# Attention and a two-layer expert on one core: every engine's queue of the opening written out by hand, and per-tile exponentials for heads 4 to 7

## The chip, the cores and the metric

The kernel runs on one core of a Trainium2 chip. The metric is device time in microseconds (us), from runs of the whole program. The engines named here are TensorE (PE, its weight loads PEld), VectorE (DVE), ScalarE (ACT), GpSimd (POOL) and SyncE (SP, which issues all the DMAs). Each engine works through its own queue in order and meets the others at semaphores.

## What is computed

Windowed attention over 8 batches of 8 heads (576 positions, head dimension 64), with a plain window of 32 keys in heads 0 to 3 of a batch and a dilated one (every 4th of 128 keys) in heads 4 to 7. Its output, 4608 tokens by 512, goes through a two-layer expert with a piecewise activation. Everything is float32.

```
scores = scale * q @ k^T;  masked to the head's window
attn = exp(scores - max);  attn = attn / (sum(attn) + 1e-09)
x = (attn @ v) as (4608, 512)
h = x @ w_in                                  # 512 -> 2048
g = h where h >= 1, 0 where h <= -1, else (h + 1)^2 / 4
out = g @ w_out                               # 2048 -> 512
```

## The kernel before

Sixty-four heads are counted through all batches (head 8 is batch 1, head 0). The queries of a head are cut into 6 tiles of 96, each against 128 keys, so a head has 6 score tiles of 96x128. Heads 0 to 15 take their scores from the float32 matmul (`scores_pair`, L187, two heads at a time), later heads from operands split into a rounded part and a rest (`scores_split`, L215; `split`, L129, makes the parts on ScalarE, VectorE and GpSimd). `reduce` (L174, instructions at L176) adds the mask and takes the lowest value on VectorE, `exp` (L248) is one ScalarE exponential a tile with its sum, `whole` (L288) does it for a head at once: subtraction on GpSimd, one ScalarE exponential over 96x768, sum on VectorE. Then come the reciprocal, the scaling by it on GpSimd or VectorE, the transposes and `values` (L349), whose results are stored as a rounded part xh and a rest xl.

The expert works in 144 steps: 9 tiles of 512 tokens times 16 blocks of 128 hidden units. Step s runs `layer1` (L391, 12 matmuls of 128x512), then VectorE and ScalarE make the activation as gh and gl, and two steps later `layer2` (L426, 12 matmuls) adds it into four accumulators. `layer1` writes one of two PSUM banks (tag h), so step s needs gl of step s-2 to be finished. After the last block of a token tile four copies (ScalarE and VectorE in turn) leave the accumulators through three buffers, and four stores leave on SP's queue (L447). Weights arrive as 64-bit words and are turned into a rounded part and a rest by `weights` (L109): two ScalarE passes, a join on VectorE (L121), a rounding copy on ScalarE (L126), a difference on GpSimd (L127). All 32 blocks are converted in the first token tile.

The order: TensorE's and SP's queues follow the program text (`manual_schedule`, L553); for the other three a scheduler with priorities and a simulated time line decides (`high_priority`, `issue_after`). Attention of heads 8 and up is dealt out between the steps by `place` (L453): two slots `u` a step. From head 16 on every pair of heads takes eight steps of the stream. The split operands qs and kk, and the loaded qr and kr of these heads, have one buffer each, so head n+1's load waits for head n's split, and its split for head n's last score matmul.

```
        for s in range(len(steps) + lag):
            ...
            if s == 2:
                acc[0] = ps.tile([128, DM], F32, tag="acc0", name="acc0_0")
                spin(14, acc[0])
```

`spin` (L155) runs matmuls on a constant; nobody reads them.

Of the kernel before, what the change touches and what calls it, by code (L numbers as in the profile page):

```python
# [23 lines left out]
F32 = mybir.dt.float32  # L24
# [12 lines left out]
TOK = 512  # L37
# [6 lines left out]

@with_exitstack
def body(ctx, tc, q, k, q2, k2, v, mask, eye, w_in, w_out, out):
# [14 lines left out]
    heads = {}  # L61
# [3 lines left out]
    spare = [f"{w}{f}" for f in range(NF // 2, NF) for w in ("wi", "wo")]  # L65

    def borrow(name):
        return pool.tile([128, 2 * DM], F32, tag=spare.pop(0), name=name)

    def load_pair(n):  # L70

        if 0 < n < H:
            qr, kr = borrow(f"qr{n}")[:, :S], borrow(f"kr{n}")[:, :KPAD]
        else:
            tags = ("qs", "kk") if n % 4 else ("qr", "kr")
            qr = pool.tile([128, S], F32, tag=tags[0], name=f"qr{n}")
# [24 lines left out]
    wi, wo, raws = {}, {}, {}  # L101

    def fetch(f, src, name):

        raw = pool.tile([128, 2 * DM], U32, tag=f"{name}{f}", name=f"{name}_raw{f}")
        nc.sync.dma_start(out=raw, in_=src[:, f].bitcast(U32))
        raws[name, f] = raw

    def weights(f, w, name):  # L109

        raw = raws.pop((name, f))
        words = raw.rearrange("p (n x) -> p n x", x=2)
        low, high = words[:, :, 0], words[:, :, 1]
        m = pool.tile([128, DM], U32, tag="m", name=f"{name}_m{f}", bufs=3)
# [70 lines left out]
    def scores_pair(n, t0, t1):  # L187

        pair = (n, n + 1)
        plain = n % H < H // 2  # L190
        svs = []
        for m in pair:
            if t0 == 0:
                begin(m)
            tag, bufs = bank(n)
            sp = ps.tile([128, 512], F32, tag=tag, name=f"s{m}_{t0}", bufs=bufs)
            svs.append(sp[:QT, : (t1 - t0) * 128].rearrange("p (t j) -> p t j", j=128))
            if m == 0 and t0 == 0:
                spin(11, sp)
# [15 lines left out]
    def scores_split(n, t0):  # L215
# [3 lines left out]
        if t0 == 0:  # L219
            begin(n)  # L220
# [462 lines left out]
```

## Time and profile before

| | us |
|---|---|
| median of 3 runs | 923.7 (923.62 to 924.82) |
| the profiled execution | 924.36 |
| span of the profile, first to last instruction | 922.6 |
| TensorE busy | 903.7 (98%) |
| VectorE, ScalarE, GpSimd busy | 671.2, 493.9, 240.6 |

The profiled execution is 0.66 us above the median, and 1.76 us of it lie outside the span. TensorE's busy time counts the spins too, and its ends are modelled, so the share alone says little: what matters is when the stream of expert steps begins, and where it has gaps.

### The profile page before, as it was taken

What the parts mean: (1) busy time and instruction counts of PE and PEld (TensorE: products, weight loads), DVE (VectorE), ACT (ScalarE), POOL (GpSimd) and SP (SyncE); (2) the same over time, 40 slices, a digit from 0 to 9 for tenths busy, and PEclk for the clock granted to TensorE, in tenths of its full rate; (3) what the DMA queues carried; (4) which work ended last, traced back from release to release, by engine and by line L of the source; (5) the groups of instructions that cost most, each with busy time, mean ns of one, the idle gap of its engine ahead of it and who ended that gap; (6) DMA issues with size and microseconds to landing.
All of it is one profiled execution on the core that took longest, in us unless ns stands there. A gap on an engine that the chain in (4) does not pass through costs nothing.

```text
span 922.6 us, 14390 instructions
## 1 busy us (share of the span) xinstructions
PE 903.7 (98%) x4866; PEld 740.7 (80%) x4866; DVE 671.2 (73%) x1966; ACT 493.9 (54%) x1352; POOL 240.6 (26%) x155
## 2 busy tenths in 40 slices
PE   7889999999999999999999999999999999999997
PEld 6677788888888888888888888888888888888886
DVE  6887778878888888788888888888888643334333
ACT  6898875555555556555555565555555422222221
POOL 4575552222222322222222222222222000000000
PEclk9999999999999999999999999999999999999999
DMA  9981013221132223211322223222321010001001
GB/s 350 407 312 45 1 27 105 82 71 57 58 116 71 70 70 117 57 54 59 116 71 70 71 73 101 57 71 71 116 70 44 1 46 1 1 1 46 1 1 47
DMA packets 31018, 73.87 MB, mean 80 GB/s; under 512 B 3520, under 2 KB 3808, under 8 KB 30944
## 3 DMA queue, kind: packets, MB, share of 16 engines
q1 hardware_dynamic: 30944, 72.94, 24.4%
q8 instruction: 39, 0.64, 0.3%
q14 instruction: 35, 0.29, 0.1%
HBM read 63.49 MB, written 9.44 MB: 79 GB/s over the span
## 4 chain that ended last, share of the span: by engine, by line
PE 89%; ACT 3%; POOL 2%; DVE 2%; issue 2%; DMA 1%; DVEq 0%; POOLq 0%; ACTq 0%
PE acc L434 41%; PE h L398 40%; PE s L225 4%; PE o L360 3%; ACT c L250 1%; POOL wi L127 1%; DMA wi_raw<-w_in 1%; POOL wo L127 1%; POOL c L286 1%; DVE c L176 1%; DVE c L293 0%; PE s L159 0%; DVE xl L345 0%; ACT wi_raw L120 0%; PE s L202 0%
## 5 line engine op out<-in xcount | busy, mean ns | idle before, releaser
L434 PE MATMUL acc<-wo,gh 128*128 128x512 f32 x1152 | 382.7, 393 | 0.0
L398 PE MATMUL h<-xh,wi 128*128 128x512 f32 x1152 | 357.3, 391 | 1.2 <-DVE gl L421 1.2
L434 PEld LDWEIGHTS acc<-wo,gh 128*128 128x128 f32 x1152 | 216.5, 188 | 47.2
L398 PEld LDWEIGHTS h<-xh,wi 128*128 128x128 f32 x1152 | 209.1, 188 | 39.9 <-DVE gl L421 1.4
L434 PE MATMUL acc<-wo,gl 128*128 128x512 f32 x576 | 225.2, 391 | 0.0
L398 PE MATMUL h<-xl,wi 128*128 128x512 f32 x576 | 224.3, 389 | 0.0
L138 POOL TENSOR_TENSOR kk<-kr,kk 128x608 fp32r<-128x608 f32 x48 | 94.8, 1975 | 413.1 <-ACT kk L134 403.0
L250 ACT ACTIVATE c<-c 96x128 f32<-96x128 f32 x330 | 129.0, 393 | 121.3 <-DVE c L176 121.3
L415 ACT ACTIVATE y<-y,consts 128x512 f32<-128x512 f32 x144 | 104.2, 724 | 116.3 <-DVE y L412 116.2
L418 ACT CAST gh<-h 128x512 fp32r<-128x512 f32 x144 | 84.4, 586 | 122.4 <-PE acc L434 118.6
L412 DVE TENSOR_SCALAR y<-h 128x512 f32<-128x512 f32 x144 | 99.2, 689 | 54.7 <-PE h L398 54.3
L417 DVE TENSOR_TENSOR h<-h,y 128x512 f32<-128x512 f32 x144 | 100.5, 698 | 49.7 <-ACT y L415 48.5
L421 DVE TENSOR_TENSOR gl<-h,gh 128x512 fp32r<-128x512 f32 x144 | 98.7, 686 | 40.9 <-ACT gh L418 40.9
L398 PEld LDWEIGHTS h<-xl,wi 128*128 128x128 f32 x576 | 108.2, 188 | 23.1
L434 PEld LDWEIGHTS acc<-wo,gl 128*128 128x128 f32 x576 | 108.2, 188 | 19.6
L301 DVE STREAM_TRANSPOSE pt<-c 32x192 f32<-32x192 f32 x288 | 106.0, 368 | 7.0 <-POOL c L286 3.7
L244 DVE TENSOR_TENSOR c<-s,msk 96x256 f32<-96x256 f32 (+1 forms) x168 | 61.4, 377 | 35.5 <-PE s L225 34.5
L286 POOL TENSOR_TENSOR c<-c 96x768 f32<-96x768 f32 x56 | 83.4, 1490 | 14.4 <-DVE c L285 14.4
L176 DVE CUSTOM_DVE_ANT_0 c<-s,c 96x128 f32<-96x128 f32 x288 | 70.6, 280 | 1.0
L250 ACT ACTIVATION_READ_ACCUMULATOR c<-c 96x1 f32 x330 | 62.3, 189 | 0.0
L225 PEld LDWEIGHTS s<-kk,qs 128*96 128x96 f32 x288 | 46.3, 161 | 15.6 <-issue 0.2
L344 ACT CAST xh<-o 128x288 fp32r<-128x288 f32 (+8 forms) x112 | 38.5, 384 | 36.8 <-PE o L360 22.9
(57 smaller groups left out, 638.7 us busy)
## 6 DMA issues: line engine op xcount, KB each, us to landing
kr<-k_in SPq DMA_DIRECT2D x56, 304.0 KB, 3.3
qr<-q_in SPq DMA_DIRECT2D x56, 288.0 KB, 2.8
vt<-v_in SPq DMA_DIRECT2D x32, 384.0 KB, 3.9
out<-out SPq DMA_DIRECT2D x36, 256.0 KB, 3.3
wi_raw<-w_in SPq DMA_DIRECT2D x16, 512.0 KB, 9.5
wo_raw<-w_in SPq DMA_DIRECT2D x16, 512.0 KB, 9.5
msk<-mask_in SPq DMA_DIRECT2D x1, 144.0 KB, 4.3
ident<-eye_in SPq DMA_DIRECT2D x1, 36.0 KB, 4.4
```

Of the source, the lines that this page charges most:

```text
L138: nc.gpsimd.tensor_tensor(out=kk[:, 1], in0=hd["kr"], in1=kk[:, 0].bitcast(F32), op=ALU.subtract)
L225: PE.matmul(out=sv[:, t - t0], lhsT=hd["qs"][:, t * QT : (t + 1) * QT], rhs=hd["ks"][:, :, t * QT : t * QT + 128], start=True, stop=True,)
L250: last["act"] = nc.scalar.activation(out=c[:, t], in_=c[:, t], func=AF.Exp, bias=st[:, 0, t : t + 1], scale=-1.0, accum_out=st[:, 1, t : t ...
L286: nc.gpsimd.tensor_tensor(out=c, in0=c, in1=spread(st[:, 2]), op=ALU.mult)
L301: nc.vector.transpose(out=pt[r : r + 32, :, 32 * g : 32 * g + 32], in_=c[32 * g : 32 * g + 32, :, r : r + 32],)
L398: PE.matmul(out=hp, lhsT=wi[f][:, w, 128 * c : 128 * c + 128], rhs=x[:, c], start=c == 0 and i == 0, stop=c == NC - 1 and i == len(terms) - 1,
L412: nc.vector.tensor_scalar(out=y, in0=hp, scalar1=-1.0, scalar2=1.0, op0=ALU.max, op1=ALU.min)
L415: nc.scalar.activation(out=y, in_=y, func=AF.Square, bias=half_t, scale=0.5)
L417: activated = nc.vector.tensor_tensor(out=hp, in0=hp, in1=y, op=ALU.max)
L418: copied = nc.scalar.copy(out=gh, in_=hp)
L421: nc.vector.tensor_tensor(out=gl, in0=hp, in1=gh.bitcast(F32), op=ALU.subtract)
L434: PE.matmul(out=acc[m], lhsT=g[:, r], rhs=wo[f][:, w], start=f == 0 and i == 0, stop=f == NF - 1 and i == len(terms) - 1,)
```

## The change

A string, `OPENING`, lists some 980 operations by short names, and `play` issues them in that order with all five engines under `manual_schedule`: loads (`q0`, `wi3`), score tiles (`S0.1`), reduces (`r0.1`), exponentials (`e0.1`), conversions of weights (`a`, `b`, `j`, `h`, `l` before a block's name), quarters of `layer1` (`A2.0`) and of `layer2` (`B0.0`), spins (`W3`). It reaches through `layer1` of step 17 and `layer2` of step 15, the last of the first token tile. From there (step 18) the loop goes on as before. Functions that issued several instructions are cut into one for each. Besides:

- heads 4 to 7: six exponentials of one tile each on ScalarE in place of GpSimd's subtraction and one exponential over the head; their bias is the tile's lowest score, they take no sum, and VectorE's sum over the head stays;
- head 3's scaling goes from GpSimd to VectorE (`by_vector`);
- fixed homes for borrowed buffers (`home`), another order of the loads, other spins (28 in six places, the last ahead of the values of head 2, none ahead of step 2).

```diff
+OPENING = """
+k0 q0 msk q4 q2 k2 v0 k4 k6 S0.0 q6 S1.0 S0.1 S1.1 r0.0 S0.2 wi0 r0.1 S1.2 e0.0 S0.3 r1.0 S1.3 S0.4 r0.2 wi3
...
+j17 B15.3 S17.4 g17 m17.4 ck18 r17.5 r17.4 d17 e17.5 cl18 e17.4 i17 R17 n17 k19 q18 cq18 cs18 q19
...
-    def exp(n, t):
+    whole_pass = (8, 9, 10, 12, 14)
+    sum_apart = (4, 5, 6, 7)
+    by_vector = (3, 5, 7)
+
+    def exp(n, t=None):
         c, st = heads[n]["c"], heads[n]["st"]
-        last["act"] = nc.scalar.activation(
-            out=c[:, t],
-            in_=c[:, t],
-            func=AF.Exp,
-            bias=st[:, 0, t : t + 1],
-            scale=-1.0,
-            accum_out=st[:, 1, t : t + 1],
-        )
+        if t is None:
+            nc.scalar.activation(out=c, in_=c, func=AF.Exp, scale=-1.0)
+        else:
+            total = {} if n in sum_apart else dict(accum_out=st[:, 1, t : t + 1])
+            nc.scalar.activation(
+                out=c[:, t], in_=c[:, t], func=AF.Exp, bias=st[:, 0, t : t + 1], scale=-1.0, **total
+            )
...
+    def summed(n):
+        c, st = heads[n]["c"], heads[n]["st"]
+        nc.vector.tensor_reduce(out=st[:, 1], in_=c, op=ALU.add, axis=mybir.AxisListType.X)
...
+    def normalised(n):
+        c = heads[n]["c"]
+        engine = nc.vector if n in by_vector else nc.gpsimd
+        engine.tensor_tensor(out=c, in0=c, in1=spread(factor(n)), op=ALU.mult)
...
+    operations = {
+        "q": load_q, "k": load_k, "v": load_v,
+        "S": scores, "m": masked, "r": lowest, "z": shifted, "e": exp, "u": summed,
+        "i": guarded, "R": inverse, "n": normalised, "T": transpose_pe, "p": kept, "t": turned,
+        "V": weighted, "x": x_high, "l": x_low,
+        "cq": q_high, "ck": k_high, "cs": q_low, "cl": k_low,
+        "A": layer1, "y": clamped, "s": squared, "j": activated, "g": g_high, "d": g_low, "B": layer2,
+        "W": lambda times: spin(times, step_bank(0)),
+    }
...
+    ordered = {engines.PE, engines.SP, engines.Activation, engines.DVE, engines.Pool}
+    with tc.manual_schedule(engines=ordered):
+        for token in OPENING.split():
+            play(token)
+    lag = 2
+    with tc.manual_schedule(engines={engines.PE, engines.SP}):
+        for u in range(2 * start - 1):
+            slots.pop(u, None)
+        run(2 * start - 1)
+        for s in range(start, len(steps) + lag):
```

The order on ScalarE in the opening, first before the change. The rows run from the last exponentials of heads 2 and 3 to the end of heads 4 to 7 (c is a head's scores, t a transposed tile in PSUM, o the values, raw and m a block of weights).

```order
L250 ACTIVATE c3_176<-c3_176 96x128
L292 ACTIVATE c4_222<-c4_222 96x768
L328 COPY pts_xh_71<-t0_0_307 128x384
L292 ACTIVATE c5_224<-c5_224 96x768
L328 COPY pts_xh_71<-t1_0_322 128x384
L344 CAST xh0_367<-o0_0_360 128x288
L344 CAST xh0_367<-o0_1_371 128x224
L328 COPY pts_xh_71<-t2_0_384 128x384
L292 ACTIVATE c6_264<-c6_264 96x768
L344 CAST xh1_380<-o0_1_371 128x64
L328 COPY pts_xl_72<-t3_0_394 128x384
L292 ACTIVATE c7_266<-c7_266 96x768
```

And in the change:

```order
L354 ACTIVATE c2_place_150<-c2_place_150 96x128 x2
L178 ACTIVATE wi0_m_276<-wi0_raw_113 128x512
L354 ACTIVATE c5_place_180<-c5_place_180 96x128
L354 ACTIVATE c4_place_177<-c4_place_177 96x128
L354 ACTIVATE c2_place_150<-c2_place_150 96x128 x2
L354 ACTIVATE c4_place_177<-c4_place_177 96x128
L354 ACTIVATE c6_place_213<-c6_place_213 96x128
L354 ACTIVATE c4_place_177<-c4_place_177 96x128
L354 ACTIVATE c6_place_213<-c6_place_213 96x128 x5
L438 COPY pts_xh_71<-t0_0_286 128x384
L438 COPY pts_xh_71<-t1_0_312 128x384
L184 ACTIVATE wi0_raw_113<-wi0_raw_113 128x512
```

The four exponentials over a whole head, each of which waited for GpSimd, became tiles of several heads mixed, and the first conversions of weights stand among them.

The second place is the end of the first token tile on SP's queue. Before (qr and kr are queries and keys of a head, out0_0 to out0_3 the four stores of the first token tile):

```order
L87 DMA qr18_1622<-q2_in 128x576
L88 DMA kr18_1623<-k2_in 128x608
L96 DMA vt16_1710<-v_in 128x768
L87 DMA qr19_1763<-q2_in 128x576
L88 DMA kr19_1764<-k2_in 128x608
L447 DMA out<-out0_0_1800 128x512
L447 DMA out<-out0_1_1806 128x512
L447 DMA out<-out0_2_1812 128x512
L447 DMA out<-out0_3_1818 128x512
```

In the change:

```order
L149 DMA kr18_1670<-k2_in 128x608
L574 DMA out<-out0_0_1778 128x512
L574 DMA out<-out0_1_1788 128x512
L574 DMA out<-out0_2_1795 128x512
L574 DMA out<-out0_3_1802 128x512
L149 DMA kr19_1824<-k2_in 128x608
L135 DMA qr18_1826<-q2_in 128x576
L135 DMA qr19_1830<-q2_in 128x576
```

The load of head 18's queries moved from ahead of the four stores to behind them. On TensorE the last score matmul of head 17 (`S17.4`) moved too: before it stood ahead of `layer1` of step 17, in the change it stands behind the last matmul of `layer2` of step 15, right ahead of head 18's first score matmul.

The third place is VectorE's queue there. Before (qs is the split of the queries, pt a transposed head, gl the rest of the activation):

```order
L244 TENSOR_TENSOR c17_1697<-s17_4_1751,msk_64 96x256
L421 TENSOR_TENSOR gl1_0_1727<-h1_0_1712,gh1_0_1726 128x512
L176 ISA c17_1697<-s17_4_1751,c17_1697 96x128
L135 TENSOR_TENSOR qs18_1757<-qr18_1622,qs18_1757 64x576
L285 RECIPROCAL c17_1697<-c17_1697 96x6
L412 TENSOR_SCALAR y1_1_1789<-h1_1_1776 128x512
L444 COPY out0_1_1806<-acc0_1_769 128x512
L417 TENSOR_TENSOR h1_1_1776<-h1_1_1776,y1_1_1789 128x512
L301 STREAM_TRANSPOSE pt1_68<-c17_1697 32x6x32 x6
L244 TENSOR_TENSOR c18_1827<-s18_0_1828,msk_64 96x256
L444 COPY out0_3_1818<-acc0_3_777 128x512
```

In the change:

```order
L532 TENSOR_SCALAR y17_1782<-h1_1_1748 128x512
L571 COPY out0_1_1788<-acc0_1_747 128x512
L538 TENSOR_TENSOR h1_1_1748<-h1_1_1748,y17_1782 128x512
L571 COPY out0_3_1802<-acc0_3_764 128x512
L326 TENSOR_TENSOR c17_1726<-s17_4_1805,msk_64 96x256
L263 ISA c17_1726<-s17_4_1805,c17_1726 96x128
L549 TENSOR_TENSOR gl17_1809<-h1_1_1748,gh17_1808 128x512
L385 RECIPROCAL c17_1726<-c17_1726 96x6
L401 STREAM_TRANSPOSE pt1_68<-c17_1726 32x6x32 x6
L224 TENSOR_TENSOR qs18_1812<-qr18_1826,qs18_1812 64x576
L326 TENSOR_TENSOR c18_1841<-s18_0_1842,msk_64 96x256
```

The split of head 18's queries moved behind the fourth copy of the outputs, behind head 17's last two tiles and behind head 17's six transposes.

## Rows read from the trace of the kernel before

**Rows 1.** The page's first line.
```profile
span 922.6 us, 14390 instructions
```

**Rows 2.** Busy time by stretches, all engines. [...]
```profile
49.80:157.20 107.40, 104.05 (x592) 83.75 (x591) 83.62 (x198) 87.60 (x204) 60.36 (x42) 1.00 0.25 82
42.00:45.00 3.00, 1.01 (x8) 0.70 (x8) 3.00 (x21) 2.26 (x7) 3.00 (x3) 1.00 1.03 401
45.00:46.00 1.00, 1.00 (x7) 0.95 (x6) 1.00 (x2) 1.00 (x5) 0.97 (x1) 0.64 1.02 406
46.00:48.00 2.00, 2.00 (x11) 2.00 (x11) 2.00 (x11) 2.00 (x5) 1.05 (x1) 0.50 1.05 418
48.00:49.00 1.00, 1.00 (x8) 1.00 (x7) 1.00 (x2) 1.00 (x3) 0.41 (x1) 0.66 0.99 397
157.20:900.00 742.80, 742.80 (x3827) 610.32 (x3826) 542.99 (x1559) 365.24 (x1035) 155.03 (x91) 1.00 0.20 61
```

**Rows 3.** The same view for ScalarE alone. Columns: stretch, length, busy us and instructions, clock of TensorE, DMA share, GB/s.
```profile
5.00:45.00 40.00, 30.65 (x96) 1.00 1.03 401
```

**Rows 4.** The timeline of TensorE from 45 to 58 us. Columns: start, length in us, engine, line, operation, out<-in, array, shapes, how many, and in brackets the idle time before and what ended it.
```profile
45.05 5.02 PE L159 MATMUL acc<-consts 128*128 128x128 f32 x28
49.82 0.71 PE L398 MATMUL h<-xh,wi 128*128 128x512 f32 x2
...
57.22 0.73 PE L398 MATMUL h<-xh,wi 128*128 128x512 f32 x2 [1.18 <-DVE gl L421]
```

**Rows 5.** The timeline of ScalarE, columns as in rows 4: first exponentials, one over a whole head, gh of step 0, and a copy of 128x128 with the instruction that follows it.
```profile
6.65 0.40 ACT L250 ACTIVATE c<-c 96x128 f32<-96x128 f32 x1 [4.64 <-DVE c L176]
...
7.05 0.39 ACT L250 ACTIVATE c<-c 96x128 f32<-96x128 f32 x1
7.34 0.19 ACT L250 ACTIVATION_READ_ACCUMULATOR c<-c 96x1 f32 x1
7.44 0.39 ACT L250 ACTIVATE c<-c 96x128 f32<-96x128 f32 x1
...
22.64 0.84 ACT L292 ACTIVATE c<-c 96x768 f32<-96x768 f32 x1
...
45.64 0.56 ACT L418 CAST gh<-h 128x512 fp32r<-128x512 f32 x1
...
69.21 0.25 ACT L344 CAST xh<-o 128x128 fp32r<-128x128 f32 x1
69.35 0.48 ACT L328 COPY pt<-t 128x384 f32<-128x384 f32 x1
```

**Rows 6.** The timeline of GpSimd, columns as in rows 4: the subtractions of `whole` for two heads, and the scaling of a head at 118.50 us.
```profile
14.89 2.89 POOL L291 TENSOR_TENSOR c<-c 96x768 f32<-96x768 f32 x2
...
118.50 1.92 POOL L286 TENSOR_TENSOR c<-c 96x768 f32<-96x768 f32 x1
```

**Rows 7.** Line 121, the join of the two halves of a weight, on VectorE: how many, then shortest, median and longest in ns, first and last start.
```profile
L121 DVE SCALAR_TENSOR_TENSOR wi_m<-wi_m,wi_raw x16: 675/693/2605, 28.3 to 119.6; 128x512 uint32<-128x512 uint32 x16
```

**Rows 8.** The timeline of VectorE around the longest of them, columns as in rows 4.
```profile
119.61 2.60 DVE L121 SCALAR_TENSOR_TENSOR wi_m<-wi_m,wi_raw 128x512 uint32<-128x512 uint32 x1
```

**Rows 9.** The timeline of all engines from 155 to 172 us, around the end of the first token tile and head 18, columns as in rows 4. At 157.17 stands head 18's first score matmul.
```profile
155.32 0.59 ACT L446 COPY out<-acc 128x512 f32<-128x512 f32 x1 [0.88 <-PE acc L434]
...
155.99 5.32 SPq L447 DMA_DIRECT2D out<-out  x4
...
157.17 0.40 PE L225 MATMUL s<-kk,qs 128*96 128x256 f32 x2
...
160.25 0.69 DVE L444 COPY out<-acc 128x512 f32<-128x512 f32 x1 [0.33 <-DMA out<-out]
...
160.86 0.68 DVE L421 TENSOR_TENSOR gl<-h,gh 128x512 fp32r<-128x512 f32 x1
...
161.67 0.28 DVE L176 CUSTOM_DVE_ANT_0 c<-s,c 96x128 f32<-96x128 f32 x1
...
162.24 0.39 ACT L250 ACTIVATE c<-c 96x128 f32<-96x128 f32 x1
...
164.02 0.41 DVE L244 TENSOR_TENSOR c<-s,msk 96x256 f32<-96x256 f32 x1
...
164.68 0.28 DVE L176 CUSTOM_DVE_ANT_0 c<-s,c 96x128 f32<-96x128 f32 x1
...
165.60 0.76 DVE L135 TENSOR_TENSOR qs<-qr,qs 64x576 fp32r<-64x576 f32 x1
...
166.25 0.39 ACT L250 ACTIVATE c<-c 96x128 f32<-96x128 f32 x1
...
166.76 0.21 ACT L284 ACTIVATE c<-c 96x6 f32<-96x6 f32 x1
...
167.11 0.19 DVE L285 RECIPROCAL c<-c 96x6 f32<-96x6 f32 x1
...
167.67 1.46 POOL L286 TENSOR_TENSOR c<-c 96x768 f32<-96x768 f32 x1
...
169.16 2.28 DVE L301 STREAM_TRANSPOSE pt<-c 32x192 f32<-32x192 f32 x6 [0.32 <-POOL c L286]
```

**Rows 10.** The stores and the loads of queries: us from issue to landing, shortest, median, longest (first the line of the stores, then that of the loads).
```profile
DMA to landing us min/median/max: 2.0/3.3/5.2
DMA to landing us min/median/max: 2.6/2.8/4.6
```

More of the change, by code (lines that the diff above doesn't have):

```diff
@@ L99, in load_values @@
             heads[n + j]["vt"] = vt[:, j]
[L101 to L114, printed above, removed]
+    source = {"wi": w_in, "wo": w_out}
@@ L185, in reduce @@
         )
[L187 to L199, printed above, removed]
-        for t in range(t0, t1):
-            for m, sv in zip(pair, svs):
-                PE.matmul(
-                    out=sv[:, t - t0],
-                    lhsT=heads[m]["qs"][:, t * QT : (t + 1) * QT],
-                    rhs=heads[m]["ks"][:, t * QT : t * QT + 128],
-                    start=True,
-                    stop=True,
-                )
-        with tc.high_priority(offset=100 if n >= H else 0):
-            for t in range(t0, t1):
-                for m, sv in zip(pair, svs):
-                    which = (0 if t == 0 else 2) if plain else t % 3
-                    reduce(m, t, (sv[:, t - t0], msk[:, which]))
+    scored = {}
@@ new lines, in scores @@
+    def scores(n, t):
+        begin(n)
+        if n >= native:
+            return scores_split(n, t)
+        t0 = 0 if t < 4 else 4
+        if (n, t0) not in scored:
+            tag, bufs = bank(n - n % 2)
+            scored[n, t0] = ps.tile([128, 512], F32, tag=tag, name=f"s{n}_{t0}", bufs=bufs)
+            if n == t0 == 0:
+                spin(9, scored[n, t0])
+        PE.matmul(
+            out=scored[n, t0][:QT, (t - t0) * 128 : (t - t0 + 1) * 128],
+            lhsT=heads[n]["qs"][:, t * QT : (t + 1) * QT],
+            rhs=heads[n]["ks"][:, t * QT : t * QT + 128],
+            start=True,
+            stop=True,
+        )
@@ L387, in body, with weighted @@
-    gs = {}
-    hps = {}
-    def layer1(t, f, cs=range(NC), bank=("h", 2)):
-        xh, xl = xtile(t)
-        if cs[0] == 0 and (t, f) not in hps:
-            hps[t, f] = ps.tile([128, TOK], F32, tag=bank[0], name=f"h{t}_{f}", bufs=bank[1])
-        hp = hps[t, f]
-        terms = [(w, x, c) for c in cs for w, x in ((0, xh), (1, xh), (0, xl))]
-        for i, (w, x, c) in enumerate(terms):
+    valued = {}
+    def weighted(n, part):
+        op = valued[n, part] = ps.tile([128, 512], F32, tag="att", name=f"o{n}_{part}", bufs=2)
+        for i in range(3):
+            for j in range(2):
+                PE.matmul(
+                    out=op[64 * j : 64 * j + 64, i * QT : (i + 1) * QT],
+                    lhsT=heads[n + j]["vt"][:, 3 * part + i],
+                    rhs=pt_of(n + j)[:, 3 * part + i],
+                    start=True,
+                    stop=True,
+                )
@@ L614, in body @@
             run(2 * s)
-            while l2 <= s - lag and l2 < len(steps):
-                layer2(*steps[l2])
-                l2 += 1
+            for m in range(TOK // 128):
+                layer2(s - lag, m)
             run(2 * s + 1)
```

634 lines of the change are left out of this document (317 added, 317 removed), and 3 rows, old and new, of the table home.

## The prediction, on record before the change was run

> **What bounds the kernel now.** I read the page first. Of the span [rows 1] TensorE is busy 98%, but its share counts spins, so I looked at stretches. From 157.20 to 900 us it is busy 742.80 of 742.80 us at a granted clock of 1.00 [rows 2]. Nothing on another engine can shorten that part. From head 18's first score matmul (157.17 [rows 9]) on, TensorE's queue holds the same instructions in the same order before and after the change. So the change is worth what it does to the moment at which that matmul starts, if the same work follows it without gaps.
>
> What lies ahead of that moment has two parts. In the **opening** the stream begins at 49.82, when `layer1` of step 2 starts [rows 4]. Ahead of it stand 28 spins from 45.05 on: TensorE has nothing to do until gl of step 0 frees the bank of step 2. The clock, 1.00 until 45, is 0.64, 0.50 and 0.66 in the following stretches [rows 2]; between 42 and 45 TensorE was busy 1.01 of 3 us. In the **stream** from 49.80 to 157.20 it is busy 104.05 of 107.40 us, so the gaps sum to 3.35 us [rows 2]; the largest stands at 57.22, 1.18 us, ended by VectorE's gl [rows 4].
>
> **Part 1, the opening on ScalarE.** Between its first exponential at 6.65 [rows 5] and gh of step 0 at 45.64 ScalarE never rests long: in 5 to 45 it is busy 30.65 us [rows 3], so 9.35 are idle, 1.65 of them before 6.65. That leaves 7.7 us of idle time that a better order could fill. By the two queue listings the change puts ahead of gh of step 0:
> - six more conversion passes (three first ones, two second ones, one rounding copy), at the 0.56 of a 128x512 cast [rows 5]: +3.36;
> - two summed exponentials fewer, at their pitch of 0.39 (7.05 to 7.44 [rows 5]): -0.78;
> - four whole-head exponentials fewer, at 0.84 in their row [rows 5], some 0.75 as a pitch since neighbours overlap: -3.0;
> - 24 tile exponentials without a sum. Their pitch is not in the trace. From below, a copy of 128x128 is followed by the next instruction after 0.14 (69.21 to 69.35); from above, an exponential's sum read-out starts 0.29 after it (7.05 to 7.34 [rows 5]). I take 0.20, nearer the copy because both only stream one tile: +4.8, with ends of 3.4 and 7.0.
>
> The sum is +4.4. If all idle time were filled, gh of step 0 would start at 45.64 - 7.7 + 4.4 = 42.3. After it come gh (0.5) and gl (0.6), after which step 2 may start: **43.5**, with ends of 42.0 (exponentials at 0.14) and 46.5 (exponentials at 0.29, 2.2 later, and 0.8 of idle time kept). The gain is 49.82 - 43.5 = 6.3, between 3.3 and 7.8. This holds the 1.7 us that the spins lost to the low clock (0.36 x 1 + 0.50 x 2 + 0.34 x 1), since they end where the wait ends.
>
> GpSimd loses four subtractions, 2.89 us for two [rows 6], and one scaling; I cost that at nothing, for ScalarE's longer list hides it. Head 3's scaling goes to VectorE; GpSimd's 1.46 for one [rows 9] is its upper bound. I cost it at nothing too, since the tiles of heads 4 to 7 on ScalarE go on beside it; without that cover step 2 would come up to 1.5 later, still before 46.5. VectorE's sums stay. The other order of the loads moves no bytes between stretches that I can price: the DMA engines are full (share 1.03 in 42 to 45 [rows 2]) either way.
>
> **Part 2, gaps in the stream.** With step 0 to 15 laid out by hand I take 1.5 us of the 3.35 to remain: gain 1.85, between -0.5 (a late weight or join adds a gap) and 3.35. Parts 1 and 2 together: 8.15.
>
> **Part 3, the seam at the end of the first token tile.** In the change SP's queue holds head 18's queries behind the four stores and behind head 19's keys, TensorE's holds `S17.4` right ahead of `S18.0`, and VectorE's holds the split of head 18's queries behind the fourth copy, head 17's last two tiles and its six transposes. The query split has one buffer, so it may not start before `S17.4`; `S18.0` waits for it. Everything behind `S18.0`, `layer1` of step 18 first, is queued behind that wait on TensorE.
>
> I count from E, the end of the last `layer2` matmul of step 15 (157.17 before). All rows are rows 9. The fourth copy waits for the first store to land (5.32 for four stores; it started at 160.25) and the next instruction on VectorE follows at 160.86, so E + 3.69. Then the chain of head 17's last tiles:
> - mask to second reduce, 164.02 to 164.68: E + 4.35;
> - reduce to second exponential, 161.67 to 162.24: E + 4.92;
> - that to the guarding add, 166.25 to 166.76: E + 5.43;
> - add to reciprocal, 0.35, and the reciprocal's 0.19: E + 5.97;
> - GpSimd's scaling to the first transpose, 167.67 to 169.16: E + 7.46;
> - six transposes, 2.28: E + 9.74;
> - the query split, 0.76: E + 10.5.
>
> TensorE works some 0.2 of it on the two matmuls of `S17.4` (0.40 for a pair in its row, from which I take a half, since their ends overlap what follows), so it loses **10.3**. The other limb is shorter: the fourth store is issued at about E + 4.1, head 19's keys and head 18's queries by E + 4.9, the landing takes 2.8 [rows 10], ScalarE's cast ends by about E + 8.3, and VectorE's own queue comes later. Before, this cost nothing, as head 18's split stood far ahead. If the first store lands in 2.0 and not the 4.26 of this trace (155.99 to 160.25), the wait is 2.3 shorter; if in 5.2 [rows 10], 0.9 longer: 8.0 to 11.2. Nothing hides it: TensorE's next work is behind the wait.
>
> **Part 4, the clock after the seam.** After the thin stretch of 42 to 45 the clock was 0.50 although TensorE was full [rows 2], and the recovery cost 1.7 us. A gap of 10 us is longer than that stretch's idle time of 2. I take 1.7, with ends of 0 and 1.7 (the only fall in the rows).
>
> **Sum.** -8.15 + 10.3 + 1.7 = +3.85. The profiled execution's 924.36 becomes 928.2; the median of the runs is 0.66 below that execution, so 923.7 + 3.85 = **927.5**. With the ends of one term at a time, 925.0 to 930.5.
>
> **The rivals.**
> - *The opening pays less.* A join takes VectorE 0.675 us at the shortest and 2.605 at the longest [rows 7]; the longest starts at 119.61 [rows 8], just over a microsecond after a scaling of 1.92 began on GpSimd [rows 6]. The change puts more joins early, beside GpSimd's scalings and differences, and each may cost up to 1.9. With exponentials at 0.29 (2.2 more than taken) and 0.8 of a stretched join on the path, step 2 starts at 46.5 and the stream keeps its gaps: -3.3 + 10.3 + 1.7 = +8.7, so 932.4. For it speaks the long join; against it that GpSimd loses four subtractions. Chance 0.20. [...]
> - *The seam is cheaper.* The clock stays up, or the first store lands early, or both: 925.8 with the first alone, 923.5 with both. For it speaks that the landing varies from 2.0 to 5.2 [rows 10]. Chance 0.18.
> - *Faster: the seam does not hold TensorE.* If `S18.0` got its split while `layer2` of step 15 still ran, parts 3 and 4 fall away: 923.7 - 8.15 = 915.5. This is decided by whether the split must wait for `S17.4`: any split finished before E makes the wait zero. Against it speaks the queue of VectorE, where six transposes of a head whose scores are not yet computed stand ahead. Even a gap cut to 6 us by shorter links leaves a gain of 0.45 with the clock's fall, and 2.15 without it. Chance 0.10.
> - *Forecast.* Chance 0.52.
>
> **How the numbers follow.** A measurement of this kernel can tell 0.2%, about 1.85 us, from no change. The range takes in the forecast's ends, the cheaper seam down to 923.0 and the dear opening to 932.0; left out are the 0.10 of the faster rival and the upper half of the first, which together are some 0.2. Slower by over 0.2% (above 925.5): nearly all of the forecast's 0.52, the first rival's 0.20 and a part of the second's, 0.75 with what lies between; within 0.2%: the rest of the second rival, 0.13; faster: 0.12, the third rival with a little for an opening that pays more than its bound.
>
> **What would show it.** In the changed kernel's profile: `layer1` of step 2 near 43.5; gaps of about 1.5 us between it and head 17's last score matmul; a gap on TensorE of 8 to 11 us right ahead of head 18's first score matmul, near 149, ended by VectorE's qs; behind it a granted clock of 0.5 for some 2 us; then TensorE busy without a gap to the end. Starts of neighbouring bare exponentials 0.20 apart prove or refute the price that decides part 1. The prediction is wrong if that gap is missing or under 5 us, if step 2 starts before 42 or after 46.5, or if new gaps in the stream exceed 4 us.

## The result and the profile after

The changed kernel takes 932.16 us (931.38 to 933.64, 4 runs) against 924.0 (4 runs, the three of the table above among them): a ratio of 1.0089, interval 1.0072 to 1.0106, so 8.2 us slower. Forecast were 927.5 and a range to 932.0. The direction was right, the size was not: 3.85 were forecast, and the time lies just above the range. One execution of E7 below took 1572.06 us at a mean clock of 0.668; it is left out of that run's median.

The page's first line, and the busy time by stretches of the changed kernel. Columns, here and in [rows 2]: stretch, its length, then for PE, PEld, DVE, ACT and POOL the busy us and the number of instructions, the granted TensorE clock as a share of full speed, the DMA engines' share and GB/s.

```profile
span 930.5 us, 14387 instructions
```

```profile
5.00:15.00 10.00, 7.18 (x72) 5.41 (x72) 6.42 (x56) 7.38 (x35) 0.00 (x0) 1.00 1.00 382
15.00:21.00 6.00, 5.41 (x37) 4.82 (x36) 4.26 (x32) 4.90 (x21) 2.93 (x2) 0.50 1.03 403
5.00:45.00 40.00, 33.92 (x322) 27.13 (x322) 32.68 (x170) 34.96 (x114) 15.59 (x11) 0.91 0.90 338
50.70:156.00 105.30, 104.03 (x588) 83.42 (x588) 86.45 (x201) 84.69 (x200) 56.43 (x40) 1.00 0.28 101
155.00:164.00 9.00, 0.63 (x4) 0.32 (x2) 5.98 (x16) 3.77 (x10) 2.93 (x2) 0.68 0.50 178
164.00:168.00 4.00, 3.93 (x11) 3.19 (x12) 0.93 (x5) 0.88 (x4) 0.00 (x0) 0.50 0.27 78
170.00:900.00 730.00, 730.00 (x3770) 599.72 (x3769) 534.74 (x1540) 361.86 (x1026) 155.37 (x91) 1.00 0.19 60
```

Three things are to be seen. The opening has a stretch at half the clock (15 to 21) which the kernel before did not have. The stream has shrunk its gaps, from 3.35 us [rows 2] to 105.30 - 104.03 = 1.27, of which 0.36 (155.64 to 156.00) are already the gap that follows: some 0.9 are left. And TensorE all but stands still from 155 to 164, with half the clock behind it.

**The opening**, TensorE first (columns as in [rows 4]):

```profile
6.30 0.46 PE L287 MATMUL s<-kr,qr 64*96 64x128 f32 x4 [0.72 <-DVE c L263]
...
12.91 0.67 PE L287 MATMUL s<-k_place,q_place 64*96 64x128 f32 x6 [1.00 <-DVE c_place L263]
...
13.98 1.11 PE L287 MATMUL s<-k_place,q_place 64*96 64x128 f32 x12 [0.40 <-DVE c_place L263]
...
15.68 2.16 PE L287 MATMUL s<-k_place,q_place 64*96 64x128 f32 x16 [0.59 <-DVE c_place L263]
...
50.74 0.73 PE L522 MATMUL h<-xh,wi 128*128 128x512 f32 x2 [0.53 <-DVE gl L549]
```

Score matmuls wait here for reduces of the same PSUM bank: `OPENING` writes `r0.0` ahead of `S0.2`, both in one bank, and `S0.2` starts at 6.30 after a wait of 0.72 us. At 15.68 sixteen matmuls take 2.16 us at a clock of 0.50; in E5 below the same sixteen take 1.60 at 1.00. The last row is `layer1` of step 2: 50.74, 0.92 later than before [rows 4] and 7.2 later than forecast. VectorE's last reduce of heads 0 to 7, and its work at the end of step 0 (join of wo1, clamp, maximum, gl):

```profile
22.82 0.28 DVE L263 CUSTOM_DVE_ANT_0 c_place<-s,msk 96x128 f32<-96x128 f32 x1
...
43.12 2.38 DVE L188 SCALAR_TENSOR_TENSOR wo_m<-wo_m,wo_raw 128x512 uint32<-128x512 uint32 x1
...
45.53 0.68 DVE L532 TENSOR_SCALAR y<-h 128x512 f32<-128x512 f32 x1
...
48.39 0.69 DVE L538 TENSOR_TENSOR h<-h,y 128x512 f32<-128x512 f32 x1
...
50.01 0.68 DVE L549 TENSOR_TENSOR gl<-h,gh 128x512 fp32r<-128x512 f32 x1
```

GpSimd, subtraction of head 8 and difference of wi3, beside that join:

```profile
42.24 1.47 POOL L360 TENSOR_TENSOR c_place<-c_place 96x768 f32<-96x768 f32 x1
43.67 1.28 POOL L199 TENSOR_TENSOR wi<-wi_m,wi 128x512 fp32r<-128x512 f32 x1
```

And ScalarE, three bare exponentials (without a sum) and gh of step 0 (at 45.64 before [rows 5]):

```profile
19.29 0.97 ACT L354 ACTIVATE c_place<-c_place 96x128 f32<-96x128 f32 x3
...
49.12 0.58 ACT L545 CAST gh<-h 128x512 fp32r<-128x512 f32 x1 [0.65 <-DVE h L538]
```

In the kernel before, the last reduce of heads 0 to 7 stood at 18.61, and gl of step 0 was done at 47.89 while the spins went on to 49.82:

```profile
18.61 0.28 DVE L176 CUSTOM_DVE_ANT_0 c<-s,msk 96x128 f32<-96x128 f32 x1
...
47.21 0.68 DVE L421 TENSOR_TENSOR gl<-h,gh 128x512 fp32r<-128x512 f32 x1
```

**The seam**, all engines, columns as in [rows 9]. At 155.23 stands `S17.4`, at 164.07 `S18.0`:

```profile
154.00 3.20 SPq L574 DMA_DIRECT2D out<-out  x4
...
155.23 0.40 PE L302 MATMUL s<-kk,qs 128*96 128x256 f32 x2
...
156.15 0.69 DVE L571 COPY out<-acc 128x512 f32<-128x512 f32 x1
...
157.44 1.47 POOL L228 TENSOR_TENSOR kk<-kr,kk 128x608 fp32r<-128x608 f32 x1 [13.91 <-ACT kk L220]
...
158.68 0.19 DVE L385 RECIPROCAL c<-c 96x6 f32<-96x6 f32 x1 [0.37 <-ACT c L379]
158.94 0.34 SPq L149 DMA_DIRECT2D kr<-k_in  x1
158.95 1.46 POOL L390 TENSOR_TENSOR c<-c 96x768 f32<-96x768 f32 x1
159.32 4.95 SPq L135 DMA_DIRECT2D qr<-q_in  x2
160.45 2.28 DVE L401 STREAM_TRANSPOSE pt<-c 32x192 f32<-32x192 f32 x6 [1.57 <-POOL c L390]
162.46 0.67 ACT L217 CAST qs<-qr 128x576 fp32r<-128x576 f32 x1 [3.81 <-DMA qr<-q_in]
163.16 0.76 DVE L224 TENSOR_TENSOR qs<-qr,qs 64x576 fp32r<-64x576 f32 x1 [0.43 <-ACT qs L217]
...
164.07 0.71 PE L302 MATMUL s<-kk,qs 128*96 128x256 f32 x2 [8.43 <-DVE qs L224]
```

The gap is there, where and as the prediction had it, ended by VectorE's qs. The two limbs of the wait can be followed: VectorE's transposes end at 162.73, and on the other limb GpSimd's key split of head 18 frees the key buffer at 158.91, head 19's keys are issued at 158.94, head 18's queries behind them at 159.32, and ScalarE's cast of them can start at 162.46.

The spans differ by 930.5 - 922.6 = 7.9. By place: step 2 starts 0.92 later; from there to the last `layer2` of step 15 it takes 155.23 - 50.74 = 104.49 against 157.17 - 49.82 = 107.35, so -2.86 (some 0.4 of it `S17.4`, which moved behind it); the seam adds 8.84; from `S18.0` to the start of the last matmul it takes 761.52 against 759.41 (the matmul starts at 925.59 and 916.58), +2.11, most of it the low clock; and the last stores end 1.11 sooner behind it. Together 7.90.

### The profile page after: what moved, and what is told of

It reads as the page before. It is cut to its first block, busy times and chain, and to the rows that moved or that the text cites. A ratio compares the mean times of both kernels' runs of the same rounds, so it can differ in the third digit from the quotient of the medians.

```text
span 930.5 us, 14387 instructions
## 1 busy us (share of the span) xinstructions
PE 908.0 (98%) x4856; PEld 743.1 (80%) x4856; DVE 675.6 (73%) x1967; ACT 497.4 (53%) x1372; POOL 233.2 (25%) x150
## 4 chain that ended last, share of the span: by engine, by line
PE 93%; DVE 3%; ACT 2%; DMA 1%; issue 0%; POOL 0%; SPq 0%; DVEq 0%; ACTq 0%
PE acc L561 42%; PE h L522 42%; PE s L302 4%; PE o L456 3%; PE s L287 1%; DVE c_place L263 1%; PE t L432 1%; DVE c L263 0%; DMA msk<-mask_in 0%; DVE xl L497 0%; DMA qr<-q_in 0%; ACT xh L492 0%; DVE wo_m L188 0%; DVE pt L401 0%; DMA out<-out 0%
## 5 line engine op out<-in xcount | busy, mean ns | idle before, releaser
L354 ACT ACTIVATE c<-c 96x128 f32<-96x128 f32 x318 | 124.4, 392 | 119.1 <-DVE c L263 118.9
L302 PE MATMUL s<-kk,qs 128*96 128x256 f32 x288 | 57.8, 284 | 8.4 <-DVE qs L224 8.4
L354 ACT ACTIVATION_READ_ACCUMULATOR c<-c 96x1 f32 x318 | 59.6, 187 | 0.0
```

The lines of the kernel that those rows point to most:

```text
L302: PE.matmul(out=split_view(n, t0)[:, t - t0], lhsT=hd["qs"][:, t * QT : (t + 1) * QT], rhs=hd["ks"][:, :, t * QT : t * QT + 128], start=Tr ...
L354: nc.scalar.activation(out=c[:, t], in_=c[:, t], func=AF.Exp, bias=st[:, 0, t : t + 1], scale=-1.0, **total)
```

## Experiments

Each has the kernel before beside it on the same chip (924.64 us in E1 to E4, 924.29 in E5 to E8, 924.25 in E9 to E11, 925.06 in E12). Ratios are to that.

**E1, the seam moved.**

```diff
-... B13.2 k18 i16 ... A17.1 m17.0 A17.2 r17.2 r17.0 e17.2 A17.3 r17.1 r17.3 e17.0 B15.0 e17.1 y17 e17.3 B15.1
-s17 B15.2 j17 B15.3 S17.4 g17 m17.4 ck18 r17.5 r17.4 d17 e17.5 cl18 e17.4 i17 R17 n17 k19 q18 cq18 cs18 q19
+... B13.2 k18 q18 i16 ... A17.2 S17.4 r17.0 ck18 e17.2 A17.3 r17.1 cq18 e17.3 cl18 cs18 m17.4 e17.0 r17.4 B15.0
+e17.1 y17 r17.5 B15.1 s17 e17.4 B15.2 e17.5 j17 B15.3 g17 d17 i17 R17 n17 k19 q19
```

> The changed kernel, with its seam reordered alone: head 18's queries are loaded ahead of the four stores, head 17's last score matmul stands ahead of the last quarter of layer1 of step 17, and both splits of head 18 stand ahead of head 17's last tiles. Theory (the loss is the wait at the seam): the gap of 8.43 us ahead of head 18's first score matmul goes, and with it the 1.0 us that the stretch behind it lost at a low clock (764.43 before against 766.43 in the changed kernel from that matmul to the end, less its own waits); 932.2 - 9.4 = 922.8, so 1.2 under the kernel before. Rival (the wait only uncovers another one, the fourth copy's wait for the first store or VectorE's backlog): a new gap of 3 us or more ahead of layer1 of step 18 or 19, and a time of 926 or more.

Measured: 924.87 us, ratio 0.9996 (0.9985 to 1.0007). The gap is gone: TensorE is busy in all of 5 us from 155 to 160, at a clock of 1.00, and no new one took its place. From the change's ratio to this it is 0.93%, 8.6 us. The 1.2 under the kernel before did not come in the median: the times reach from 922.33 to 926.86, and the profiled execution (925.51) had its clock near 0.50 from 9 to 23 us and step 2 at 54.13. Ten of the eleven executions stand in the order of their mean granted clock, from 922.33 at 0.996 to 925.86 at 0.990; the eleventh, 926.86, had 0.998. So where the clock fell least this kernel is some 2 us under the kernel before. That scatter, in an opening which this edit does not touch, led to E5 and E6.

**E2, the load alone.**

```diff
-e16.5 B13.2 k18 i16 ... n17 k19 q18 cq18 cs18 q19
+e16.5 B13.2 k18 q18 i16 ... n17 k19 cq18 cs18 q19
```

> The changed kernel with one load moved: head 18's queries are issued on SP's queue behind its keys, ahead of the four stores. Theory of the prediction (VectorE's chain sets the seam, the transfer is the shorter limb): next to nothing, the query split starts right behind the six transposes, which ended at 162.73, and not at 163.16; 0.4 us, 931.8. Rival (the transfer sets it, and VectorE's chain has slack): the gap of 8.43 us shrinks by 2 us or more, 930 or less.

Measured: 934.08 us, ratio 1.0100 (1.0084 to 1.0115), with an opening that ended later still (step 2 at 54.83). At the seam itself the rival is right: VectorE's query split and `S18.0`,

```profile
163.35 1.78 DVE L224 TENSOR_TENSOR qs<-qr,qs 64x576 fp32r<-64x576 f32 x1 [0.37 <-ACT qs L217]
...
165.29 0.71 PE L302 MATMUL s<-kk,qs 128*96 128x256 f32 x2 [5.54 <-DVE qs L224]
```

The gap is 5.54 instead of 8.43. The split no longer stands behind the transposes: the scheduler, which orders VectorE behind the written list, put it ahead of them once its data came early. So this run does not test VectorE's chain by itself. It shows that 2.9 us of the gap hung on the transfer, and that the order of the transposes hung on it too. Why the shorter gap did not shorten the time is not shown: two of the four executions took 934.09 and 934.27 at a mean clock of 0.994, where the changed kernel took 931.38.

**E3, spins in the gap.**

```diff
-j17 B15.3 S17.4 g17 m17.4
+j17 B15.3 S17.4 W36 g17 m17.4
```

> The changed kernel with 36 spins behind head 17's last score matmul; at 0.215 us each they fill 7.7 of the 8.43 us of TensorE's gap at the seam and change nothing else. If the clock's fall behind the gap is a loss of its own: the granted clock stays at 1.00 from 165 to 170 us (0.65 in the changed kernel), and the time is 1.0 us lower, 931.2. If the idle time is all of it, or the spins hold up the work behind them: 932.2 or more.

Measured: 932.24 us, ratio 1.0083 (1.0061 to 1.0104); the medians tell nothing, with times from 929.74 to 934.65. The profile does, with its step 2 at 50.64, close to the changed kernel's 50.74 (each of the 36 spins is recorded as two matmuls):

```profile
155.37 8.20 PE L248 MATMUL h<-consts 128*128 128x128 f32 x72
```

```profile
160.00:165.00 5.00, 4.69 (x38) 4.40 (x38) 3.57 (x9) 0.67 (x1) 0.56 (x1) 1.00 0.38 124
165.00:170.00 5.00, 5.00 (x25) 4.11 (x24) 2.48 (x11) 2.42 (x9) 0.00 (x0) 1.00 0.14 48
```

The clock stays up, and from `S18.0` to the start of the last matmul it takes 759.85 us, not 761.52: the fall behind the gap costs 1.67.

**E4, the kernel before without its spins ahead of step 2.**

```diff
                 acc[0] = ps.tile([128, DM], F32, tag="acc0", name="acc0_0")
-                spin(14, acc[0])
```

> The kernel before without the spins ahead of layer1 of step 2, nothing else changed on TensorE. In its trace gl of step 0 ends at 47.89, but the spins, at a granted clock of 0.50, last until 49.82. If the spins themselves held the stream up: layer1 of step 2 starts at 48.0 and the time falls by 1.9, to 922.1. If the spins keep the clock up for the stream behind them: without them the clock stands at 0.5 for the first 3 us of the stream, 1.5 to 1.9 us are given back, and the time is 924 as before. For the prediction, which credited the change with 6.3 us in the opening, the first case means that 1.9 of these were the spins' own overrun.

Measured: 924.73 us, ratio 1.0002 (0.9994 to 1.0011): no difference. A stretch of its trace and the start of step 2:

```profile
48.00:54.00 6.00, 3.58 (x8) 2.81 (x9) 5.35 (x15) 6.00 (x14) 1.91 (x2) 0.50 1.04 407
```

```profile
50.42 1.22 PE L398 MATMUL h<-xh,wi 128*128 128x512 f32 x2 [2.83 <-DVE gl L421]
```

gl is done at 50.37 (this execution's first reduce came 1.26 later than before's, 7.58 to 6.32), and step 2 follows at once, at half the clock. The spins did hold the stream up, and they paid for it with the clock (1.00 from 49 to 54 before, 0.50 from 48 to 54 here). The second case was right.

**E5, score matmuls ahead of the reduces.** On top of E1; each engine's order stays as it was, for example

```diff
-S0.0 q6 S1.0 S0.1 S1.1 r0.0 S0.2 wi0 r0.1 S1.2 e0.0 S0.3 r1.0 S1.3 S0.4 r0.2
+S0.0 q6 S1.0 S0.1 S1.1 S0.2 S1.2 S0.3 S1.3 r0.0 wi0 r0.1 e0.0 r1.0 S0.4 r0.2
```

> E1's kernel (the changed kernel with its seam moved) with the score matmuls of heads 0 to 7 written ahead of the first reduce of their PSUM bank; every engine's own order stays as it was, only the waits between TensorE and VectorE go (a score matmul written behind a reduce of the same bank waits for it, and the reduce for the matmul ahead of it). Theory (those waits make TensorE idle between 5 and 16 us and its clock fall there: 0.50 from 15 to 21 us in the changed kernel, from 9 to 23 in E1's): the granted clock stays at 1.00 up to 25 us, the last score tile of heads 0 to 7 comes some 3 us earlier than in the changed kernel (20.98), layer1 of step 2 starts at 46 to 48 and not at 50.74 (54.13 in E1's), and the time is 919 to 921.5. Rival (ScalarE and the loads set the opening, TensorE's waits there are slack): step 2 stays at 50 or later and the time within 1 of E1's.

Measured: 920.12 us (919.89 to 921.06), ratio 0.9956 (0.9944 to 0.9967). The stretch that was slow, the last reduce of heads 0 to 7, and step 2:

```profile
15.00:21.00 6.00, 5.83 (x62) 5.12 (x58) 5.85 (x45) 6.00 (x25) 3.23 (x3) 1.00 1.03 400
```

```profile
20.16 0.28 DVE L258 CUSTOM_DVE_ANT_0 c_place<-s,msk 96x128 f32<-96x128 f32 x1
```

```profile
48.58 0.73 PE L517 MATMUL h<-xh,wi 128*128 128x512 f32 x2 [0.52 <-DVE gl L544]
```

The theory holds, though step 2 is a little later than the 46 to 48 expected. From the first reduce to the last it takes 13.1 us (7.08 to 20.16), in the changed kernel 16.9 (5.95 to 22.82), before 12.3 (6.32 to 18.61). Step 2 follows the last reduce after 28.4 us here and 27.9 in the changed kernel, so the reduces' delay went through undiminished. No run here leaves these waits out, so whether they are needed is not shown; the list's order changes how often they are met: among the first 24 score matmuls there are two in the changed kernel (0.72 and 0.38 us) and none here.

**E6, spins instead**, on top of E1.

```diff
-r0.0 S0.2 ... e0.0 S0.3 ... r4.0 S4.2 ... r5.1 S5.3 ... wi4 S7.4
+r0.0 W3 S0.2 ... e0.0 W1 S0.3 ... r4.0 W4 S4.2 ... r5.1 W1 S5.3 ... wi4 W2 S7.4
```

> E1's kernel with 11 more spins in five places of the opening, ahead of score matmuls that waited for VectorE between 5 and 16 us. The waits stay, only TensorE's idle time is filled. If the clock's fall is what costs in the opening: the clock stays at 1.00 to 25 us, step 2 starts 2 to 4 us earlier than in E1's profile (54.13), the time is 921 to 923. If the waits themselves set the pace: the clock stays up, but step 2 comes no earlier than 50.7, and the time is 923 to 925.

Measured: 921.9 us, ratio 0.9974 (0.9963 to 0.9984). The first case holds: clock 1.00 throughout, first to last reduce 15.2 us (6.63 to 21.79), step 2 at 50.19. So with the waits kept and the clock up it takes 15.2, with the waits cut too 13.1, with neither 16.9 in the changed kernel and 18.8 in E1's profile (6.77 to 25.53). By the ratios spins alone gain 2.0 us on E1 (0.9996 to 0.9974), which is the clock's part, and E5's order 1.7 more.

**E7, the end of step 0 first.** On top of E1.

```diff
-z8 awi4 wo11 jwo1 A0.2 bwi4 A0.3 lwi3 wi6 e8 S10.0 l6.1.1 y0 hwo1 S11.0 ... S11.2 s0 r11.0 ... r10.2 awi5 j0 ... S11.5 d0 s1 r10.5 A2.0
+z8 awi4 wo11 A0.2 bwi4 A0.3 lwi3 wi6 e8 S10.0 l6.1.1 y0 s0 S11.0 ... r11.0 j0 g0 ... d0 e11.0 jwo1 hwo1 lwo1 ... A1.3 A2.0 y1 ...
```

> E1's kernel with the end of step 0 moved ahead: on VectorE its clamp, its maximum and gl stand ahead of the join of wo1 and of most reduces of heads 10 and 11, on TensorE layer1 of step 2 ahead of the last score tiles of those heads. In the changed kernel that join stood ahead of the clamp and took 2.38 us instead of 0.69, and five reduces stood ahead of the maximum; the last quarter of layer1 of step 0 ended at 44.3 and gl at 50.7. Theory (this detour sets step 2): from the end of step 0's last quarter to layer1 of step 2 it takes 3.4 us instead of 6.4, and the time falls by 3 against E1, to 921.5 to 922. Rival (what is put off comes due in the stream: weights of step 1 late, reduces late): new gaps before 100 us take 1.5 us or more of it back, 923.5 or more.

Measured: 924.61 us (921.79 to 926.40, 11 runs), ratio 1.0000 (0.9988 to 1.0012).

```profile
48.13 0.73 PE L522 MATMUL h<-xh,wi 128*128 128x512 f32 x2 [0.15 <-DVE gl L549]
...
49.95 0.89 PE L287 MATMUL s<-kr,qr 64*96 64x128 f32 x8 [0.85 <-DVE c L263]
...
56.56 0.72 PE L522 MATMUL h<-xh,wi 128*128 128x512 f32 x2 [0.72 <-DVE gl L549]
```

From the last reduce (23.02) to step 2 it takes 25.1 us and not 27.9, as the theory said, and two new gaps of 1.57 take more than half of it back, as the rival said. In the time nothing is left that the scatter would show.

**E8, whole-head exponentials for heads 4 to 7**, on top of E1; so for each of the four heads:

```diff
-... r4.2 e4.0 ... n0 r4.4 S6.0 r4.5 v2 ... e4.1 wi1 ... e4.5 T1.0
+... r4.2 ... n0 r4.4 S6.0 r4.5 z4 v2 ... wi1 ... e4 T1.0
```

> E1's kernel with the exponentials of heads 4 to 7 as in the kernel before: GpSimd subtracts, ScalarE takes one exponential over the head, in place of 24 tiles (measured 0.29 us apart in the changed kernel). ScalarE loses 24 x 0.29 = 7.0 and gains 4 x 0.75 = 3.0, GpSimd gains 4 x 1.45 = 5.8. Theory of the prediction (ScalarE sets the opening): step 2 starts up to 4 us earlier than in E1's profile, 921 to 923. Rival (ScalarE waits elsewhere in the opening, and the subtraction delays heads 4 to 7 and stretches what VectorE does beside it): step 2 no earlier or later, 925 to 929.

Measured: 924.76 us, ratio 1.0005 (0.9995 to 1.0016), times from 923.25 to 929.45, the clock at 0.50 from 9 to 25 us in the profile. It decides nothing; E10 repeats it on E5.

**E9, E5's order with the change's own seam**: E5's edit made on the changed kernel, without E1's.

> The changed kernel with the score matmuls of heads 0 to 7 written ahead of the first reduce of their bank (as E5's), and its seam as it is. E5's opening ran at a clock of 1.00 throughout and its times lay within 1.2 us, so against E5 this prices the seam without the opening's scatter. Theory (the seam is 8.4 us of idle time and 1.0 of low clock, independent of when the opening ends): 920.1 + 9.4 = 929.5, and the times lie close together. Rival (part of the seam's wait comes from the late opening): under 927.

Measured: 931.57 us, ratio 1.0067 (1.0050 to 1.0085). Against E5 that is 1.11%, 10.3 us, for the seam, a little more than the 9.4 expected; the gap is 8.37 us. In this profile the clock fell again (0.57 from 15 to 21) after TensorE had waited 1.70 us at 9.42, with the same opening as E5's. So the order does not exclude the fall; it may make it rarer, since two of E5's five executions had a mean clock of 1.000 and none of E1's eleven had.

**E10, whole-head exponentials on E5**: E8's edit made on E5.

> E5's kernel (seam moved, score matmuls ahead of the reduces) with whole-head exponentials and GpSimd's subtraction for heads 4 to 7. E8 left this open, since the fall of the clock in the opening scattered its times over 6 us. If the per-tile exponentials are a gain of the change: step 2 later than 48.6 by 1 to 4 us, 921.1 to 924. If ScalarE's 4.0 us less count: 46 to 47.5 and 917 to 919. If neither sets the opening: within 0.8 of E5's 920.1.

Measured: 922.82 us, ratio 0.9978 (0.9968 to 0.9988), by the ratios 2.0 us slower than E5. Its trace shows the transposes of a head that wait for GpSimd, and step 2:

```profile
21.25 0.71 PE L353 MATMUL t<-ident,c 96*128 96x96 f32 x6 [2.03 <-POOL c L320]
```

```profile
51.17 0.74 PE L428 MATMUL h<-xh,wi 128*128 128x512 f32 x2 [0.35 <-DVE gl L450]
```

The reduces end at 19.84, a little earlier than E5's, and step 2 comes 31.3 later, not 28.4 (the clock fell from 47 to 50 us, which may be a part of that). The per-tile exponentials are a gain of the change, some 2 us, although ScalarE does more with them. The trace has the likely reason: on GpSimd two subtractions (2.89 us from 16.88) stand ahead of the scaling (19.73 to 21.20) for which those transposes wait.

**E11, the end of step 0 first, on E5**, as E7 but for

```diff
-... d0 e11.0 jwo1 hwo1 lwo1 r11.3 r10.2 ... y1 e11.1 z9 r10.3 r11.2 s1 S10.4 ... jwi4 ... awo2 j1
+... d0 e11.0 r11.3 r10.2 ... y1 e11.1 r10.3 r11.2 s1 jwo1 hwo1 lwo1 z9 S10.4 ... j1 ... jwi4 ... awo2
```

> E5's kernel with the end of step 0 moved ahead as in E7, and two of the gaps that E7 opened behind it met: the last reduces of heads 10 and 11 ahead of the join of wo1, and the maximum of step 1 ahead of the join of wi4 (stretched to 1.61 there). Theory (the detour of step 0 sets step 2, and the stream can take the work that is put off): step 2 at 46.0, new gaps under 1 us in all, 917.5 to 918.5. Rival (what is put off comes due): step 2 at 46, but gaps of 1.5 us or more before 60 us, 919.5 or more.

Measured: 923.43 us, ratio 0.9986 (0.9976 to 0.9995), by the ratios 2.8 us slower than E5.

```profile
46.12 0.73 PE L517 MATMUL h<-xh,wi 128*128 128x512 f32 x2 [0.15 <-DVE gl L544]
...
56.63 1.22 PE L517 MATMUL h<-xh,wi 128*128 128x512 f32 x2 [3.41 <-DVE gl L544]
```

The rival: step 2 at 46.12, and then 3.41 us of waiting for gl of step 1, at half the clock behind it. Work put off at step 0 was due at step 1.

**E12, spins on E5.**

```diff
-W3 S2.0 S3.0 ... S2.4 ... S6.4 ... S7.4
+W5 S2.0 W2 S3.0 ... W3 S2.4 ... W3 S6.4 ... W2 S7.4
```

> E5's kernel with 12 more spins of 0.2 us ahead of the score matmuls of heads 2 to 7 that still waited for VectorE there (0.42, 0.56, 0.58, 0.66 and 0.39 us in E5's trace). E9 has E5's opening, and its profiled execution fell to a clock of 0.50 from 15 to 22 us, after a wait of 1.70 us at 9.4, while E5's did not. If E5 escapes the fall only in executions whose first loads land early: the clock now stays at 1.00 in every profile, the times lie between 919.5 and 921, no better than E5's best (919.89) and without a tail. If the spins hold up the score matmuls behind them: step 2 later than 49.5 and 921 or more.

Measured: 920.68 us (919.12 to 922.65), ratio 0.9952 (0.9936 to 0.9968). In the profile TensorE has no wait from 5 to 21 us, the clock is 1.00 and step 2 starts at 48.17; the best time is below E5's. But the tail did not go, and 919.12 and 921.61 came at the same mean clock of 0.999, so what scatters these times is not the early fall alone. Against the kernel before on its chip it gains 0.48%, 4.4 us. E5 and E12 beat both kernels; between the two nothing is decided.

## Why the prediction was off, point by point

**What bounds the kernel: right.** From 170 us on TensorE is busy 730.00 of 730.00 us. The differences lie ahead of `S18.0`, but for the low clock right behind it and 1.11 at the last stores.

**Part 1, the opening, is the step that failed.** It forecast step 2 at 43.5, with 46.5 as the upper end; it came at 50.74. The sentence that failed is "If all idle time were filled, gh of step 0 would start at 45.64 - 7.7 + 4.4 = 42.3". It took ScalarE's list as the bound and looked at no other engine's order ahead of it. The list itself was priced well but for one term: a bare exponential takes 0.29 to the next, the upper end, not 0.20, which is 24 x 0.09 = 2.2. From its first exponential to gh of step 0 ScalarE is busy 37.75 of 42.84 us (6.28 to 49.12), before 31.29 of 38.99 (6.65 to 45.64), so the list grew by 6.46, and 4.4 + 2.2 is 6.6. The idle time was not filled: 5.09 us of the 7.70 stayed, where the sum has nothing and its upper end 0.8. What kept ScalarE waiting, and was left out:
- The reduces of heads 0 to 7 end at 22.82 instead of 18.61, 4.2 later, because score matmuls wait for reduces in their bank (0.19 to 1.00 us, six times from 5 to 16) and TensorE runs at half its clock from 15 to 21. E5 takes most of that away, E6 the clock's part. The list wrote `r0.0` ahead of `S0.2` in plain sight, and the change in the spins (28 for 33, by their calls) had no price.
- The end of step 0 on VectorE: the join of wo1 took 2.38 and not 0.69 ahead of the clamp, beside GpSimd's subtraction and difference, and reduces of heads 10 and 11 stood ahead of the maximum. E7 shows 2.8 us. The stretched join is what the first rival named, which took 0.8 for it where 1.7 came.

With the corrected price 43.5 becomes 45.7, and E11 had step 2 at 46.12. That is no proof of the sum: in E11 two conversion passes and two summed exponentials of the list stand behind gh of step 0, and ScalarE still had 3.41 us of idle time (35.23 busy of the 38.64 from 6.12 to 44.76). In E5 it had 2.55 (37.00 of the 39.55 from 7.41 to 46.96). No run filled all of it.

Also wrong there: that the spins before "end where the wait ends". gl was done 1.9 us before they ended. E4 shows that this made no difference to the time, since without them the clock was lost in the stream instead (0.50 from 48 to 54).

**Part 2: right.** 1.5 us of gaps were to remain, some 0.9 did.

**Part 3: the mechanism was right, the size and the limb were not.** `S17.4` came 8.84 ahead of `S18.0`; forecast were 10.5. The fourth copy did not wait for the first store, since the four stores of the seam landed after 2.0 to 2.1 us, where the first one had taken 4.26 in the kernel before; this is the case that the prediction priced at 2.3 less. VectorE's chain then ended at 162.73, and the transfer, called the shorter limb, ended later, at 163.13 with its cast: SP's queue had to wait for GpSimd's key split before it could issue head 19's keys, which the prediction had not on its list, and the queries stood behind them. E2 shows what hung on that.

**Part 4: right.** 1.7 forecast, 1.67 by E3. The clock at 0.50 right behind the gap was forecast for some 2 us and held for about 4.

**The first rival was the one that came true**, at 932.4 for a measured 932.16, with the stretched join but not with its place in the sum: it let the stream keep its gaps, which it did not, and started it at 46.5, when it was 50.74. The sum agreed by errors that cancel: the opening was 4.2 worse than its term, the stream 2.9 and the seam 1.5 better.

## What to carry to other kernels

When an order is written by hand across engines, the order between engines counts as much as the order on each: in the changed kernel a reduce written ahead of the next matmul into its bank was a wait in both directions (the matmul at 6.30 waited 0.72 us for a reduce, the reduce at 6.79 then 0.55 for a matmul). TensorE's short waits there came with a fall of its clock to 0.50 from 15 to 21 us; in E9 it fell after one of 1.70, in E5 it stayed at 1.00 through five of 0.39 to 0.66, and in E12, where spins filled them, at 1.00 too. Price the first engine in the chain before the last: an engine's idle time can be filled only from the moment at which its first input comes (the reduce at 5.95 and ScalarE's first exponential at 6.28 here). At a seam between a written list and a loop, look for what the list's last loads stand behind: here 8.6 us (E1) to 10.3 (E9) hung on the place of one load, one score matmul and the splits and tiles around them. The load alone took 2.9 us off the gap (E2).

## What was not expected of the hardware

The same opening runs at either clock from one execution to the next. E5 and E9 have the same instructions up to step 13; in one profile the clock stayed at 1.00, in the other it was 0.50 from 16 to 22 us. The landing of the first loads moves too: the mask was there at 5.95 us in the changed kernel, at 6.77 in E1. The first 24 score matmuls differ as well: they start at 5.06 us in both and take 2.43 us in E5, 1.80 in E9, while the granted clock reads 1.00 there in both. What makes the clock fall the two do not show, since the wait ahead of it differed too (0.42 us at 8.77 in E5, 1.70 at 9.42 in E9). Most of the scatter in E1's times goes with the clock (see there), but not all scatter does: two executions of E7 took 926.16 and 926.40 us at a mean clock of 1.000, and its fastest 921.79 at 0.998. What held those two up no profile here caught.

The stretch of a VectorE join beside GpSimd was seen again: 2.38 us (0.69 alone; the longest before was 2.60) from 43.12, until 0.55 us past the end of GpSimd's second instruction at 44.95, and a query split at 1.78 instead of 0.76 in E2, from 163.35, beside GpSimd's scaling from 163.06 to 164.52. That GpSimd's work is the cause no run here tests.
